# Four accumulator tiles of one bank each, and a rearranged start, in a Fourier-mixing and gated feed-forward kernel

## The chip, the cores and the metric

The kernel runs on one core of a Trainium2 chip. The metric is the device time of one execution in microseconds; a kernel's figure is the median of its runs. All times inside an execution are counted from the start of the profiled span.

## The reference

Eight sequences of 3008 tokens with 256 features go through a real Fourier transform over the tokens, a complex 256x256 product with bias, a soft threshold of real and imaginary part, and the inverse transform. The 24064 tokens that come out go through a feed-forward block with a sigmoid-gated unit, 256 to 2048 to 256.

```python
X = np.fft.rfft(x, axis=1)
Yr = Xr @ w_r - Xi @ w_i + b_r
Yi = Xr @ w_i + Xi @ w_r + b_i
Yr = np.sign(Yr) * np.maximum(np.abs(Yr) - lam, 0.0)   # Yi likewise, lam = 0.01
y = np.fft.irfft(Yr + 1j * Yi, n=x.shape[1], axis=1)
...
h = y @ w_in
g = h * (1.0 / (1.0 + np.exp(-1.702 * h)))
out = g @ w_out
```

The feed-forward weights come as float64, everything else is float32.

## The kernel before

**Numbers.** Most matmuls work on values split into a high and a low part of a shorter type (`fp32r`): `split` makes the high part on ACT (a cast) and the low part on DVE (a subtraction), and `mm3` multiplies high by high, high by low and low by high: lines L130, L131 and L132 of the profile. Where one factor is exact or a phase comes early ("plain"), an ordinary float32 matmul stands instead; it has two records in the trace.

**The spectral part of one batch** (`spectral`). 3008 is 64 times 47, and the transform goes in two steps. Stage A (L283, 16 blocks) transforms along 47; ACT copies each block out of PSUM (`aev`, L287) and SP stores it to a DRAM buffer `s1` (L288). Stage B (L312, 12 steps) reads rows `br` of `s1` back (L298) with a matrix `kr` from the input `kbs` (L297), transforms along 64, and ACT copies the outcome to `co`; DVE adds its two halves. Stage mix (L331) multiplies with `w_r`, `w_i` and their sum and difference (`wr`, `wd`); bias and threshold follow on DVE and ACT, and four DMAs turn the outcome into `yr`. Stage inv (L366) goes back along 64, `iev` is stored to a second DRAM buffer `s2`. At last `tokens` loads blocks `ur` of `s2` (L400), transforms back along 47 (L408) and splits the outcome into `th` and `tl`. A row of stage B needs all 16 blocks of stage A, a block of `tokens` needs all 12 steps of stage inv.

**The feed-forward part** (`Ffn`). A tile is 512 tokens; there are 47 tiles of 8 steps `q`. `up(q)` makes 12 matmuls of 512 columns into the PSUM tiles `pa` (four banks that all stages share), ACT applies the gated unit (`gb`, L440), ACT and DVE make seven combinations and their splits (`hb`, `lb`, `ht`, `lt`). `down(q)` makes 21 matmuls of 256 columns with seven combined weight blocks (a Strassen-like scheme, `ORDER`) into the accumulator `po`, one tile of four PSUM banks. After the last step `combine` reads it out with one ACT copy (L502, `o0` from bank 0) and DVE adds (L503 to L509); POOL does one add between (L507). The last tile has `combine_last` (L488 to L497), and for its last two steps plain matmuls (L477) with `gl`.

**The weights** (`weights(q)`, q from 0 to 7). POOL requests 512 KB of float64 (`wraw`, L192), and some ten ACT and DVE operations make float32 halves of it (`we`, `wm`, `wa`, then `wi_h`, `wi_l`, `wo_h`, `wo_l`).

**What sets the order.** The code is written as one program; a scheduler then sets the order on each engine by its own estimate of when each instruction could run, and every engine works its list off in order, SP its DMA requests too. `tc.issue_after(ins)` binds what stands in its block behind `ins` on `ins`'s engine alone. A tile of a pool is free again when all its readers are done. Batch 0 runs through at the start; blocks of stage A of batches 1 and 2 serve as `filler` between the first feed-forward steps; later batches are spread between the steps by a queue. `hold_clock(ins, n)` puts n matmuls with no use (L518) on PE behind `ins`. `split_constants` splits the constants `ka`, `ki`, `wf` that batches from 1 on need.

Of the kernel before, what the change touches and what calls it, by code (L numbers as in the profile page):

```python
# [9 lines left out]
F32 = mybir.dt.float32  # L10
# [4 lines left out]
AF = mybir.ActivationFunctionType  # L15
ALU = mybir.AluOpType
# [10 lines left out]
TOK, HT = 512, 256  # L27
# [78 lines left out]
def fourier_mix_then_gated_ffn(ctx: ExitStack, tc: tile.TileContext, x, w_r, w_i, b_r, b_i, w_in, w_out, pack, kbs, out):  # L106
    nc = tc.nc
# [21 lines left out]
    def mm3(ps, wh, wl, xh, xl, start=True, stop=True):  # L129
        nc.tensor.matmul(ps, lhsT=wh, rhs=xh, start=start, stop=False)  # L130
        nc.tensor.matmul(ps, lhsT=wh, rhs=xl, start=False, stop=False)  # L131
        nc.tensor.matmul(ps, lhsT=wl, rhs=xh, start=False, stop=stop)  # L132
# [5 lines left out]
    kz, fg, fk = kc[:96, 352:446], kc[:, 446:470], kc[:, 470:482]  # L138
    nlam = cst.tile([128, 1], F32, name="nlam")
    nc.vector.memset(nlam, -LAM)  # L140
    ka = cst.tile([96, 2, 96], F32R, name="ka")
    ki = cst.tile([128, 2, 2, 128], F32R, name="ki")
    bias = cst.tile([128, 2, D], F32, name="bias")
# [91 lines left out]
        else:  # L235
            split(wo_h[:, q], wo_l[:, q], t[:, 0:7])

    done_a, done_inv = [], []
    evacuated, stored, mixed, split_to = [], [], [], []


    def spectral(b, s2):
# [4 lines left out]
        xs, raw, zs, ys = {}, {}, {}, {}  # L247

        plain, plain_a = b == 0, b < 3

# [28 lines left out]
        def stage_a(q):  # L279

            ps = bank()
            if plain_a:
                done_a.append(nc.tensor.matmul(ps[:96], lhsT=ka32, rhs=xs.pop(q), start=True, stop=True).ins)  # L283
# [4 lines left out]
            stored.append(nc.sync.dma_start(s1w[:, 512 * q:512 * (q + 1)], ev).ins)  # L288

        def load_b(sp):  # L290
            if plain:
                kt = buf([128, 3, D], F32, "br0", tag=("zh", "zl")[sp % 2])
                t, k = kt[:, 0:2], kt[:, 2].rearrange("p (i n) -> p i n", i=2)
            else:
                t, k = buf2("br"), buf([128, 2, 2 * N1], F32, "kr")
            with tc.issue_after(stored[13]):
                nc.sync.dma_start(k, kbs[sp])  # L297
            nc.sync.dma_start(t, s1r[2 * sp:2 * sp + 2].rearrange("s p d -> p s d"))  # L298
            raw[sp] = t, k

        def stage_b(sp):

            ahead = 3 if plain else 1
            for n in range(0 if sp == 0 else sp + ahead, min(sp + ahead + 1, 12)):
                load_b(n)
            t, k = raw.pop(sp)
            co = buf([128, 2, 3, 128], F32, "co")
            pv = bank().rearrange("p (c v i n) -> p c v i n", c=2, v=2, i=2)
            for i in range(2):
                for c in range(2):  # L310
                    cs = slice(128 * c, 128 * c + 128)
                    nc.tensor.matmul(pv[:, c, :, i], lhsT=t[:, i, cs], rhs=k[:, i], start=True, stop=True)  # L312
# [73 lines left out]
            for n in range(4):  # L386
                load_x(n)

        return first, second, preload


    s2s, us, ytiles = {}, {}, {}
# [32 lines left out]
    class Ffn:  # L425
# [43 lines left out]

        def down(self, q):  # L470
            if q == 0:
                self.acc = ps_o.tile([128, 4, 2, HT], F32, name="po", tag="po")
            g = self.g.pop(q)
            for n, (a, t, bk, h) in enumerate(ORDER):
                start, stop = q == 0 and FIRST[bk] == n, q == NQ - 1 and LAST[bk] == n
                if not isinstance(g[t], tuple):
                    nc.tensor.matmul(self.acc[:, bk, h], lhsT=self.w32[q][:, a], rhs=g[t], start=start, stop=stop)  # L477
                else:
                    mm3(self.acc[:, bk, h], wo_h[:, q, a], wo_l[:, q, a], *g[t], start=start, stop=stop)
            if q == NQ - 1:  # L480
                (self.combine_last if self.k == NT - 1 else self.combine)()

        def combine_last(self):

            p = self.acc
            o0, o1, uv = buf2("o0"), buf2("o1"), buf2("uv")
            v = nc.vector
            nc.scalar.copy(o0, p[:, 0])  # L488
            v.tensor_tensor(uv[:, 0], p[:, 1, 0], o0[:, 0], ALU.add)
            nc.gpsimd.tensor_tensor(o0[:, 0], o0[:, 0], o0[:, 1], ALU.add)  # L490
            v.tensor_tensor(o0[:, 1], uv[:, 0], p[:, 1, 1], ALU.add)
            v.tensor_tensor(uv[:, 1], p[:, 2, 0], uv[:, 0], ALU.add)
            v.tensor_tensor(o0[:, 1], o0[:, 1], p[:, 2, 1], ALU.add)
            nc.sync.dma_start(out[self.k, :, 0], o0.rearrange("p h n -> p (h n)"))
            v.tensor_tensor(o1[:, 1], uv[:, 1], p[:, 1, 1], ALU.add)
            v.tensor_tensor(o1[:, 0], uv[:, 1], p[:, 3, 0], ALU.subtract)
            nc.scalar.dma_start(out[self.k, :, 1], o1.rearrange("p h n -> p (h n)"))  # L497

        def combine(self):
            p = self.acc  # L500
            o0, o1, uv = buf2("o0"), buf2("o1"), buf2("uv")
            nc.scalar.copy(o0, p[:, 0])  # L502
            nc.vector.tensor_tensor(uv[:, 0], p[:, 1, 0], o0[:, 0], ALU.add)  # L503
            nc.vector.tensor_tensor(uv[:, 1], p[:, 2, 0], uv[:, 0], ALU.add)
            nc.vector.tensor_tensor(o1[:, 0], uv[:, 1], p[:, 3, 0], ALU.subtract)
            nc.vector.tensor_tensor(o1[:, 1], uv[:, 1], p[:, 1, 1], ALU.add)
            nc.gpsimd.tensor_tensor(o0[:, 0], o0[:, 0], o0[:, 1], ALU.add)  # L507
            nc.vector.tensor_tensor(o0[:, 1], uv[:, 0], p[:, 1, 1], ALU.add)
            nc.vector.tensor_tensor(o0[:, 1], o0[:, 1], p[:, 2, 1], ALU.add)  # L509
            for e, o in enumerate((o0, o1)):  # L510
                nc.sync.dma_start(out[self.k, :, e], o.rearrange("p h n -> p (h n)"))

    def hold_clock(ins, count):

        with tc.issue_after(ins):
            o = ps_o.tile([128, 4, 2, HT], F32, name="po", tag="po").rearrange("p c h n -> p (c h n)")
            for _ in range(count):
                nc.tensor.matmul(o[:96, 0:446], lhsT=ka32, rhs=kc[:96, 0:446], start=True, stop=True)  # L518

# [7 lines left out]
    (first, second, _), (first1, queue, preload), (first2, queue2, _) = (spectral(b, new_s2(b)) for b in range(3))  # L527
    nextb = 2
    for n, (_, step) in enumerate(first + second):
        step()  # L530
        if n == len(first) - 1:
            later_constants()
        if n == len(first) - 1:
            hold_clock(done_a[-1], 4)
        if n == len(first) + 36:
            preload()
    with tc.issue_after(evacuated[15]):
        split_constants()
    filler = first1 + first2
    last_aev = evacuated[15]  # L540

    def fill(count):
        for _ in range(2 * count):
            if filler:
                filler.pop(0)[1]()

    def weights(q):
        with ExitStack() as held:

            for ins in ([last_aev] if q < 5 else mixed if q == 5 else first_tokens) if q else ():  # L550
                held.enter_context(tc.issue_after(ins))
            up_weights(q, q > 5)
            down_weights(q, q > 5)
# [12 lines left out]
    for u in range(3):  # L566
        load_u(u)
    with tc.issue_after(loaded[-1]):
        fill(4)
    hold_clock(done_inv[-1], 5)  # L570
    tokens_to(TOK)
    first_tokens = tuple(split_to)
    with tc.issue_after(loaded[2]), tc.issue_after(turned[-1]):
        fill(2)
    for q in range(6):
        weights(q)
    behind = total = None
    for n in range(NT * NQ):
# [4 lines left out]
            cur = Ffn(k)  # L583
        cur.up(q)
        fill(3)
        if not queue and nextb < NB:
            if nextb == 2:
                queue = queue2
            else:
                first, second, _ = spectral(nextb, new_s2(nextb))  # L590
                queue = first + [(4000, lambda: None)] + second
            nextb += 1
            total = None
# [52 lines left out]
```

## Time and profile before

| what | value |
|---|---|
| median of three runs | 2633.46 us (2631.92 to 2638.31) |
| the profiled execution, its own time | 2632.74 us |
| its span | 2630.6 us |
| PE busy in the span | 98% |
| DVE, ACT, POOL busy | 75%, 62%, 2% |
| mean granted PE clock | 0.992 of full speed |

The time of an execution is its span and some 2 us around it. A busy PE is not yet a PE at its peak: matmuls overlap in their pipeline, and at half the granted clock the same matmul is busy for longer. So the idle time of PE and the stretches at a low clock have to be read together.

### The profile page before, as it was taken

What the parts mean: (1) busy time and instruction counts of PE and PEld (TensorE: products, weight loads), DVE (VectorE), ACT (ScalarE), POOL (GpSimd) and SP (SyncE); (2) the same over time, 40 slices, a digit from 0 to 9 for tenths busy, and PEclk for the clock granted to TensorE, in tenths of its full rate; (3) what the DMA queues carried; (4) which work ended last, traced back from release to release, by engine and by line L of the source; (5) the groups of instructions that cost most, each with busy time, mean ns of one, the idle gap of its engine ahead of it and who ended that gap; (6) DMA issues with size and microseconds to landing.
All of it is one profiled execution on the core that took longest, in us unless ns stands there. A gap on an engine that the chain in (4) does not pass through costs nothing.

```text
span 2630.6 us, 42804 instructions
## 1 busy us (share of the span) xinstructions
PE 2589.7 (98%) x16520; PEld 2327.6 (88%) x16520; DVE 1967.4 (75%) x3219; ACT 1642.7 (62%) x2547; POOL 53.8 (2%) x71
## 2 busy tenths in 40 slices
PE   7899999999999999999999999999999999999998
PEld 4679999999899998999989999899998999999998
DVE  6767877777777777777777777778777777777676
ACT  5566666666666666666676666766667666655554
POOL 1000000000000000000000000000000000000000
PEclk8899999999999999999999999999999999999999
DMA  8652221111322223212241221322213122200000
GB/s 259 205 171 71 82 86 49 50 59 55 95 79 62 69 62 103 74 60 68 64 124 56 68 67 60 120 63 61 75 60 121 47 74 62 66 18 32 18 20 17
DMA packets 156075, 200.64 MB, mean 76 GB/s; under 512 B 18688, under 2 KB 105600, under 8 KB 155872
## 3 DMA queue, kind: packets, MB, share of 16 engines
q1 hardware_dynamic: 153360, 189.26, 23.7%
q0 software_dynamic: 2368, 8.39, 1.0%
q8 instruction: 130, 2.13, 0.4%
q14 instruction: 73, 0.60, 0.1%
q10 hardware_dynamic: 144, 0.26, 0.0%
HBM read 97.70 MB, written 74.97 MB: 66 GB/s over the span
## 4 chain that ended last, share of the span: by engine, by line
PE 90%; issue 7%; DMA 2%; DVE 1%; ACT 1%; POOL 0%; SPq 0%; POOLq 0%; DVEq 0%; ACTq 0%
PE pa L130 16%; PE pa L131 16%; PE pa L132 16%; PE po L130 11%; PE po L131 11%; PE po L132 11%; PE pa L408 4%; PE pa L312 3%; PE pa L283 1%; PE pa L331 1%; DMA wraw<-in_w_in 1%; DMA s<-aev 0%; PE pa L366 0%; DMA yr<-mv 0%; ACT gb L440 0%
## 5 line engine op out<-in xcount | busy, mean ns | idle before, releaser
L440 ACT ACTIVATE gb<-pa 128x512 f32<-128x512 f32 x752 | 447.0, 598 | 424.0 <-PE pa L132 421.4
L127 DVE TENSOR_TENSOR lt<-gt,ht 128x1024 fp32r<-128x1024 f32 x374 | 458.3, 1226 | 246.8 <-ACT ht L127 245.7
L130 PE MATMUL pa<-th,wi_h 128*128 128x512 f32 x1504 | 597.5, 397 | 2.9 <-ACT gb L440 2.1
L131 PE MATMUL pa<-tl,wi_h 128*128 128x512 f32 x1504 | 591.4, 393 | 0.0
L132 PE MATMUL pa<-th,wi_l 128*128 128x512 f32 x1504 | 588.1, 391 | 0.0
L127 ACT CAST ht<-gt 128x1024 fp32r<-128x1024 f32 x374 | 391.5, 1047 | 158.5 <-DVE gt L462 146.8
L131 PE MATMUL po<-lt,wo_h 128*128 128x256 f32 x1496 | 427.0, 285 | 0.0
L130 PE MATMUL po<-ht,wo_h 128*128 128x256 f32 x1496 | 425.1, 284 | 0.0
L132 PE MATMUL po<-ht,wo_l 128*128 128x256 f32 x1496 | 423.3, 283 | 0.0
L127 DVE TENSOR_TENSOR lb<-gb,hb 128x768 fp32r<-128x768 f32 x375 | 358.7, 957 | 43.2 <-ACT hb L127 41.0
L460 DVE TENSOR_TENSOR gt<-gb 128x512 f32<-128x512 f32 x374 | 261.7, 700 | 134.5 <-ACT gb L440 131.1
L127 ACT CAST hb<-gb 128x768 fp32r<-128x768 f32 x375 | 313.4, 836 | 69.2 <-PE po L132 62.3
L132 PEld LDWEIGHTS pa<-th,wi_l 128*128 128x128 f32 x1504 | 283.5, 188 | 57.3
L130 PEld LDWEIGHTS pa<-th,wi_h 128*128 128x128 f32 x1504 | 284.9, 189 | 52.0 <-ACT gb L440 3.3
L130 PE MATMUL po<-hb,wo_h 128*128 128x256 f32 x1125 | 327.5, 291 | 0.9 <-DVE o L509 0.9
L131 PEld LDWEIGHTS pa<-tl,wi_h 128*128 128x128 f32 x1504 | 284.7, 189 | 44.4 <-DVE wa L198 0.5
L131 PE MATMUL po<-lb,wo_h 128*128 128x256 f32 x1125 | 319.9, 284 | 0.0
L132 PE MATMUL po<-hb,wo_l 128*128 128x256 f32 x1125 | 319.0, 284 | 0.0
L132 PEld LDWEIGHTS po<-ht,wo_l 128*128 128x128 f32 x1496 | 285.7, 191 | 8.6 <-issue 1.7
L131 PEld LDWEIGHTS po<-lt,wo_h 128*128 128x128 f32 x1496 | 285.6, 191 | 8.7 <-issue 1.8
L130 PEld LDWEIGHTS po<-ht,wo_h 128*128 128x128 f32 x1496 | 285.5, 191 | 3.8 <-issue 1.3
L130 PEld LDWEIGHTS po<-hb,wo_h 128*128 128x128 f32 x1125 | 214.8, 191 | 10.1 <-issue 2.6
(123 smaller groups left out, 3780.0 us busy)
## 6 DMA issues: line engine op xcount, KB each, us to landing
s<-aev SPq DMA_DIRECT2D x128, 192.0 KB, 2.6
br<-s SPq DMA_DIRECT2D x96, 256.0 KB, 3.0
yr<-mv SPq DMA_DIRECT2D x384, 64.0 KB, 2.0
s<-iev SPq DMA_DIRECT2D x96, 256.0 KB, 2.3
ur<-s SPq DMA_DIRECT2D x128, 192.0 KB, 2.8
out<-o SPq DMA_DIRECT2D x93, 256.0 KB, 2.1
xr<-in_x SPq DMA_DIRECT2D x80, 192.0 KB, 3.1
kr<-in_kbs SPq DMA_DIRECT2D x84, 128.0 KB, 2.1
```

The lines of the kernel that those rows point to most:

```text
L127: return nc.scalar.copy(hi, src).ins, nc.vector.tensor_tensor(lo, src, hi.bitcast(F32), ALU.subtract).ins
L130: nc.tensor.matmul(ps, lhsT=wh, rhs=xh, start=start, stop=False)
L131: nc.tensor.matmul(ps, lhsT=wh, rhs=xl, start=False, stop=False)
L132: nc.tensor.matmul(ps, lhsT=wl, rhs=xh, start=False, stop=stop)
L283: done_a.append(nc.tensor.matmul(ps[:96], lhsT=ka32, rhs=xs.pop(q), start=True, stop=True).ins)
L312: nc.tensor.matmul(pv[:, c, :, i], lhsT=t[:, i, cs], rhs=k[:, i], start=True, stop=True)
L331: nc.tensor.matmul(ps, lhsT=z[:, 3 * c + v], rhs=wf32[v][:, c], start=c == 0, stop=c == 1)
L408: turned.append(nc.tensor.matmul(pv[:, c, 94 * j:94 * j + 94], lhsT=t[:, j, 128 * c:128 * c + 128], rhs=kz, start=True, stop=True).ins)
L440: nc.scalar.activation(o, ps.rearrange("p (h n) -> p h n", h=2), AF.Gelu_apprx_sigmoid)
L460: nc.vector.tensor_tensor(gt[:, 0:2], b12, gb[:, 0:3:2], ALU.subtract)
```

## The change

- The accumulator is four tiles of one bank, each with its own tag (`po0` to `po3`), where it was one tile of four banks. The fillers of `hold_clock` take `po0`.
- `load_b`: the first matrix of a batch is bound to a store of stage A of the same batch (number 13 of batch 0, number 15 of the others); each further matrix is bound behind the row request before it. In before all matrices were bound to batch 0's store 13.
- `preload_b`: rows 0 and 1 of batch 1 are requested when 12 or fewer filler steps are left.
- `split_constants` stands behind the last mixing operations of batch 0 (`mixed`, one on DVE and one on ACT), where it stood behind the last `aev` copy.
- `weights(1)` is bound to `aev` copy 11 in place of 15.
- 7 unused matmuls behind stage A for 4; 3 for 5 at the end of batch 0, now bound behind stage A blocks; three filler blocks for four at that place, bound behind the last stage inv; one for two after the first tokens.
- A one-element activation loads the gated unit's table at the start.

```diff
+    nc.scalar.activation(cst.tile([128, 1], F32, name="gelu_table"), nlam, AF.Gelu_apprx_sigmoid)
...
-            stored.append(nc.sync.dma_start(s1w[:, 512 * q:512 * (q + 1)], ev).ins)
+            mine.append(nc.sync.dma_start(s1w[:, 512 * q:512 * (q + 1)], ev).ins)
+            stored.append(mine[-1])
...
-            with tc.issue_after(stored[13]):
+            if sp == 0:
+                later.append(mine[13 if plain else 15])
+            with tc.issue_after(later[-1]):
                 nc.sync.dma_start(k, kbs[sp])
-            nc.sync.dma_start(t, s1r[2 * sp:2 * sp + 2].rearrange("s p d -> p s d"))
+            later.append(nc.sync.dma_start(t, s1r[2 * sp:2 * sp + 2].rearrange("s p d -> p s d")).ins)
...
+        def preload_b():
+            load_b(0)
+            load_b(1)
...
-                self.acc = ps_o.tile([128, 4, 2, HT], F32, name="po", tag="po")
+                self.acc = [ps_o.tile([128, 2, HT], F32, name="po", tag=f"po{i}") for i in range(4)]
...
-                    mm3(self.acc[:, bk, h], wo_h[:, q, a], wo_l[:, q, a], *g[t], start=start, stop=stop)
+                    mm3(self.acc[bk][:, h], wo_h[:, q, a], wo_l[:, q, a], *g[t], start=start, stop=stop)
...
-            hold_clock(done_a[-1], 4)
+            hold_clock(done_a[-1], 7)
...
-    with tc.issue_after(evacuated[15]):
+    with tc.issue_after(mixed[0]), tc.issue_after(mixed[1]):
         split_constants()
...
-            for ins in ([last_aev] if q < 5 else mixed if q == 5 else first_tokens) if q else ():
+            for ins in ([evacuated[11 if q == 1 else 15]] if q < 5 else mixed if q == 5 else first_tokens) if q else ():
...
     with tc.issue_after(loaded[-1]):
-        fill(4)
-    hold_clock(done_inv[-1], 5)
+        with tc.issue_after(done_inv[-1]):
+            fill(3)
+    hold_clock(done_a[-1], 3)
...
-        fill(2)
+        fill(1)
...
+        if preload_b and len(filler) <= 12:
+            preload_b()
+            preload_b = None
```

Lines shift by up to 12: stage A's L283 is L284 in the changed kernel, L298 is L302, L312 is L317, L366 is L371, L400 is L409, L408 is L417, L477 is L486, L518 is L527. The same instructions run as before, but for one unused matmul more and one activation in place of a second table load. What moves is seen at three places.

**SP, between stage A and stage B of batch 0.** Before: the last two stores `s_83<-aev`, the bias, five matrices (three of batch 0, two `kr` of batch 1), then four rows.

```order
L288 DMA s_83<-aev 96x512 x2
L154 DMA bias<-in_b_r 128x256
L155 DMA bias<-in_b_i 128x256
L297 DMA br_202<-in_kbs 128x256
L297 DMA br_205<-in_kbs 128x256
L297 DMA br_208<-in_kbs 128x256
L297 DMA kr<-in_kbs 128x256 x2
L298 DMA br_199<-s_83 128x2x256
L298 DMA br_202<-s_83 128x2x256
L298 DMA br_205<-s_83 128x2x256
```

The same place in the changed kernel:

```order
L289 DMA s_85<-aev 96x512 x2
L155 DMA bias<-in_b_r 128x256
L156 DMA bias<-in_b_i 128x256
L302 DMA br_204<-s_85 128x2x256
L301 DMA br_207<-in_kbs 128x256
L302 DMA br_207<-s_85 128x2x256
L301 DMA br_210<-in_kbs 128x256
L302 DMA br_210<-s_85 128x2x256
```

The first row stands right behind the bias, and each matrix behind the row before it; the two `kr` have moved far back.

**PE, from the end of batch 0 to the first feed-forward matmul.** Before: L366 is stage inv, L283 a filler block of batch 1, L518 the unused matmuls, L408 the tokens, L130 the first `up`.

```order
L366 MATMUL pa<-yr_582,kc 128x256 x2
L366 MATMUL pa<-yr_616,kc 128x256
L283 MATMUL pa<-xa,kc 96x512 x3
L366 MATMUL pa<-yr_616,kc 128x256
L518 MATMUL po<-kc 96x446 x5
L283 MATMUL pa<-xa,kc 96x512
L408 MATMUL pa<-kc,ur 128x94 x12
L283 MATMUL pa<-xa,kc 96x512 x2
L130 MATMUL pa<-th,wi_h 128x512
```

In the changed kernel:

```order
L371 MATMUL pa<-yr_587,kc 128x256 x2
L371 MATMUL pa<-yr_621,kc 128x256 x2
L284 MATMUL pa<-xa,kc 96x512 x3
L527 MATMUL po<-kc 96x446 x3
L417 MATMUL pa<-kc,ur 128x94 x12
L284 MATMUL pa<-xa,kc 96x512
L130 MATMUL pa<-th,wi_h 128x512 x2
```

The last matmul of stage inv no longer stands behind three filler blocks, no block stands ahead of the tokens, and one instead of two between them and the first `up`.

**PE, the end of the program.** Before, one accumulator (`po_27752`):

```order
L132 MATMUL po_27752<-hb_27991,wo_l_81 128x256
L477 MATMUL po_27752<-gl_27993,w32_27994 128x256 x4
L477 MATMUL po_27752<-gb_28022,w32_28040 128x256 x3
L477 MATMUL po_27752<-gl_28039,w32_28040 128x256 x4
L638 UNCONDITIONAL_BRANCH
```

In the changed kernel, with banks 0 to 3 as `po_27893` to `po_27896`:

```order
L486 MATMUL po_27895<-gb_28166,w32_28184 128x256
L486 MATMUL po_27894<-gl_28137,w32_28138 128x256
L486 MATMUL po_27894<-gl_28183,w32_28184 128x256 x2
L486 MATMUL po_27896<-gl_28137,w32_28138 128x256
L486 MATMUL po_27895<-gl_28183,w32_28184 128x256
L486 MATMUL po_27896<-gl_28183,w32_28184 128x256
L650 UNCONDITIONAL_BRANCH
```

Bank 0 takes no part in the last matmuls any more, and bank 1 ends three matmuls ahead of the end.

More of the change, by code (lines that the diff above doesn't have):

```diff
@@ L236, in down_weights @@
             split(wo_h[:, q], wo_l[:, q], t[:, 0:7])
-    done_a, done_inv = [], []
+    done_a, done_inv, later = [], [], []
     evacuated, stored, mixed, split_to = [], [], [], []
@@ L246, in spectral @@
         s2w = s2.rearrange("(s r) p j d -> s (r p j) d", r=2)
-        xs, raw, zs, ys = {}, {}, {}, {}
+        xs, raw, zs, ys, mine = {}, {}, {}, {}, []
         plain, plain_a = b == 0, b < 3
@@ L304, in stage_b @@
             for n in range(0 if sp == 0 else sp + ahead, min(sp + ahead + 1, 12)):
-                load_b(n)
+                if n not in raw:
+                    load_b(n)
             t, k = raw.pop(sp)
@@ L387, in preload @@
                 load_x(n)
-        return first, second, preload
+        def preload_b():
+            load_b(0)
+            load_b(1)
+        return first, second, preload, preload_b
     s2s, us, ytiles = {}, {}, {}
@@ L476, in down @@
                 if not isinstance(g[t], tuple):
-                    nc.tensor.matmul(self.acc[:, bk, h], lhsT=self.w32[q][:, a], rhs=g[t], start=start, stop=stop)
+                    nc.tensor.matmul(self.acc[bk][:, h], lhsT=self.w32[q][:, a], rhs=g[t], start=start, stop=stop)
                 else:
-                    mm3(self.acc[:, bk, h], wo_h[:, q, a], wo_l[:, q, a], *g[t], start=start, stop=stop)
+                    mm3(self.acc[bk][:, h], wo_h[:, q, a], wo_l[:, q, a], *g[t], start=start, stop=stop)
             if q == NQ - 1:
@@ L487, in combine_last @@
             v = nc.vector
-            nc.scalar.copy(o0, p[:, 0])
-            v.tensor_tensor(uv[:, 0], p[:, 1, 0], o0[:, 0], ALU.add)
+            nc.scalar.copy(o0, p[0])
+            v.tensor_tensor(uv[:, 0], p[1][:, 0], o0[:, 0], ALU.add)
             nc.gpsimd.tensor_tensor(o0[:, 0], o0[:, 0], o0[:, 1], ALU.add)
-            v.tensor_tensor(o0[:, 1], uv[:, 0], p[:, 1, 1], ALU.add)
-            v.tensor_tensor(uv[:, 1], p[:, 2, 0], uv[:, 0], ALU.add)
-            v.tensor_tensor(o0[:, 1], o0[:, 1], p[:, 2, 1], ALU.add)
+            v.tensor_tensor(o0[:, 1], uv[:, 0], p[1][:, 1], ALU.add)
+            v.tensor_tensor(uv[:, 1], p[2][:, 0], uv[:, 0], ALU.add)
+            v.tensor_tensor(o0[:, 1], o0[:, 1], p[2][:, 1], ALU.add)
             nc.sync.dma_start(out[self.k, :, 0], o0.rearrange("p h n -> p (h n)"))
-            v.tensor_tensor(o1[:, 1], uv[:, 1], p[:, 1, 1], ALU.add)
-            v.tensor_tensor(o1[:, 0], uv[:, 1], p[:, 3, 0], ALU.subtract)
+            v.tensor_tensor(o1[:, 1], uv[:, 1], p[1][:, 1], ALU.add)
+            v.tensor_tensor(o1[:, 0], uv[:, 1], p[3][:, 0], ALU.subtract)
             nc.scalar.dma_start(out[self.k, :, 1], o1.rearrange("p h n -> p (h n)"))
@@ L501, in combine @@
             o0, o1, uv = buf2("o0"), buf2("o1"), buf2("uv")
[L502 to L506, printed above, removed]
+            nc.scalar.copy(o0, p[0])
+            nc.vector.tensor_tensor(uv[:, 0], p[1][:, 0], o0[:, 0], ALU.add)
+            nc.vector.tensor_tensor(uv[:, 1], p[2][:, 0], uv[:, 0], ALU.add)
+            nc.vector.tensor_tensor(o1[:, 0], uv[:, 1], p[3][:, 0], ALU.subtract)
+            nc.vector.tensor_tensor(o1[:, 1], uv[:, 1], p[1][:, 1], ALU.add)
             nc.gpsimd.tensor_tensor(o0[:, 0], o0[:, 0], o0[:, 1], ALU.add)
-            nc.vector.tensor_tensor(o0[:, 1], uv[:, 0], p[:, 1, 1], ALU.add)
-            nc.vector.tensor_tensor(o0[:, 1], o0[:, 1], p[:, 2, 1], ALU.add)
+            nc.vector.tensor_tensor(o0[:, 1], uv[:, 0], p[1][:, 1], ALU.add)
+            nc.vector.tensor_tensor(o0[:, 1], o0[:, 1], p[2][:, 1], ALU.add)
             for e, o in enumerate((o0, o1)):
@@ L515, in hold_clock @@
         with tc.issue_after(ins):
-            o = ps_o.tile([128, 4, 2, HT], F32, name="po", tag="po").rearrange("p c h n -> p (c h n)")
+            o = ps_o.tile([128, 2, HT], F32, name="po", tag="po0").rearrange("p h n -> p (h n)")
             for _ in range(count):
@@ L526, in fourier_mix_then_gated_ffn @@
     assert NB > 2
-    (first, second, _), (first1, queue, preload), (first2, queue2, _) = (spectral(b, new_s2(b)) for b in range(3))
+    (first, second, *_), (first1, queue, preload, preload_b), (first2, queue2, *_) = (spectral(b, new_s2(b)) for b in range(3))
     nextb = 2
@@ L533, in fourier_mix_then_gated_ffn @@
         if n == len(first) - 1:
-            hold_clock(done_a[-1], 4)
+            hold_clock(done_a[-1], 7)
         if n == len(first) + 36:
             preload()
-    with tc.issue_after(evacuated[15]):
+    with tc.issue_after(mixed[0]), tc.issue_after(mixed[1]):
         split_constants()
     filler = first1 + first2
-    last_aev = evacuated[15]
     def fill(count):
@@ L589, in fourier_mix_then_gated_ffn @@
             else:
-                first, second, _ = spectral(nextb, new_s2(nextb))
+                first, second, *_ = spectral(nextb, new_s2(nextb))
                 queue = first + [(4000, lambda: None)] + second
```

## The prediction

> **What bounds the kernel now.** I read the page first, then windows over the span, then the order of time on PE, SP and ACT where the windows show idle PE.
>
> ```profile
> span 2630.6 us, 42804 instructions
> PE 2589.7 (98%) x16520; PEld 2327.6 (88%) x16520; DVE 1967.4 (75%) x3219; ACT 1642.7 (62%) x2547; POOL 53.8 (2%) x71
> ```
>
> PE is the bound, with some 41 us idle. The windows (stretch, length, busy time by engine, granted PE clock, DMA share, GB/s) tell where:
>
> ```profile
> 25.00:50.00 25.00, 16.07 (x60) 11.07 (x59) 18.21 (x39) 12.18 (x23) 2.17 (x3) 0.74 0.80 260
> 100.00:125.00 25.00, 20.36 (x55) 11.87 (x55) 11.30 (x25) 9.01 (x19) 0.80 (x2) 0.70 0.51 164
> 225.00:2600.00 2375.00, 2368.97 (x15467) 2160.37 (x15466) 1795.69 (x2887) 1499.42 (x2302) 39.02 (x45) 1.00 0.22 66
> 2600.00:2632.00 32.00, 23.67 (x149) 21.31 (x147) 16.51 (x28) 9.18 (x13) 0.72 (x1) 0.95 0.05 17
> ```
>
> From 225 to 2600 us PE idles 6.0 us at full clock: there is nearly nothing to be had. Two early stretches have both idle time and a clock near 0.7. Finer windows put half clock at these places:
>
> ```profile
> 34.40:44.60 10.20, 4.02 (x17) 3.90 (x18) 8.47 (x22) 2.87 (x6) 1.18 (x2) 0.50 0.86 280
> 99.20:102.60 3.40, 3.26 (x7) 1.61 (x6) 3.23 (x7) 1.60 (x3) 0.00 (x0) 0.50 0.80 255
> 112.90:126.50 13.60, 13.11 (x37) 9.25 (x38) 5.76 (x12) 6.40 (x14) 1.07 (x2) 0.50 0.52 165
> 198.20:201.60 3.40, 3.40 (x19) 3.40 (x18) 2.94 (x8) 1.90 (x3) 0.72 (x1) 0.50 0.49 147
> ```
>
> PE's order of time (start, length, work, idle before it) shows the idle ahead of each:
>
> ```profile
> 40.58 3.75 PE L312 MATMUL pa<-br 128*128 128x128 f32 x16 [8.93 <-ACT wm L199]
> ...
> 98.67 2.85 PE L366 MATMUL pa<-yr,kc 128*128 128x256 f32 x6 [2.27 <-DMA yr<-mv]
> 101.32 3.39 PE L283 MATMUL pa<-xa,kc 96*96 96x512 f32 x6
> 104.55 0.60 PE L366 MATMUL pa<-yr,kc 128*128 128x256 f32 x2
> 104.99 3.90 PE L518 MATMUL po<-kc 96*96 96x446 f32 x10
> 113.39 1.99 PE L283 MATMUL pa<-xa,kc 96*96 96x512 f32 x2 [4.50 <-DMA xa<-in_x]
> 115.18 5.27 PE L408 MATMUL pa<-kc,ur 96*128 96x94 f32 x24
> 120.24 3.62 PE L283 MATMUL pa<-xa,kc 96*96 96x512 f32 x4
> 122.88 1.42 PE L130 MATMUL pa<-th,wi_h 128*128 128x512 f32 x1
> ...
> 197.23 2.86 PE L312 MATMUL pa<-kr,br 128*128 128x128 f32 x16 [2.19 <-DMA br<-s]
> ```
>
> Idle of 2.2 us is followed within 1.2 us by a half-clock stretch of 3.4 us, 4.5 us idle by one of 13.6 us. What is saved ahead of 225 us moves all that follows, since PE is full there.
>
> **Part 1, stage A to stage B of batch 0.** SP's queue (start, length, requests):
>
> ```profile
> 29.30 0.30 SPq L288 DMA_DIRECT2D s<-aev  x1
> ...
> 30.64 1.39 SPq L297 DMA_DIRECT2D br<-in_kbs  x3
> 32.07 1.03 SPq L297 DMA_DIRECT2D kr<-in_kbs  x2
> 33.15 4.15 SPq L298 DMA_DIRECT2D br<-s  x4
> ```
>
> The last store and the first row take from issue to landing, in this order:
>
> ```profile
> DMA to landing us min/median/max: 2.8/2.8/2.8
> DMA to landing us min/median/max: 7.3/7.3/7.3
> ```
>
> The store lands at 32.1, the first row at 33.15 + 7.3 = 40.4, and PE starts at 40.58: it waits for the row, though the trace names an ACT operation that ends at the same moment. Moving five matrices behind the row saves 33.15 - 32.1 = 1.05 us of issue, and 5 x 128 KB at the 260 GB/s of that window, 2.5 us, in the queue; the two overlap only in part. I take 3: with the row at 37.4 both terms count nearly whole. The bounds are 1 (issue alone) and 5 (with the half-clock loss of 34.40:44.60, 4.02 us busy at half speed, gone too). The three more fillers cost 3 x 0.78 us of idle PE (3.90 us for 10 records, two to a matmul); they end near 34 and are covered as long as the row lands after that. The constants leave this stretch; their five casts and subtractions free ACT and DVE, and the weights move up into the gap, which is a rival below. **-3**, range -5 to +1.
>
> **Part 2, end of batch 0 to the first `up`.** ACT's order of time at this place, one constant's cast (line group: count, busy, mean ns), and the page's DMA times (KB, us to landing):
>
> ```profile
> 100.27 0.59 ACT L373 COPY iev<-pa 128x512 f32<-128x512 f32 x1 [0.58 <-ACT wm L199]
> ...
> 105.23 0.59 ACT L373 COPY iev<-pa 128x512 f32<-128x512 f32 x1 [3.85 <-issue]
> ```
>
> ```profile
> L127 ACT CAST wf_h<-wd 128x512 fp32r<-128x512 f32 x2 | 1.2, 618 | 0.2 <-DVE wd L158 0.2
> ```
>
> ```profile
> s<-iev SPq DMA_DIRECT2D x96, 256.0 KB, 2.3
> ur<-s SPq DMA_DIRECT2D x128, 192.0 KB, 2.8
> wraw<-in_w_in POOLq DMA_DIRECT2D x6, 512.0 KB, 6.3
> ```
>
> On the clock of before: the last stage-inv matmul moves ahead of three filler blocks, 104.55 - 101.32 = 3.2 us earlier, so it ends near 101.9. ACT isn't free then: the five casts now stand ahead of the last three `iev` copies, at most 5 x 0.62 = 3.1 us, about 2.5 since two of them are small. The second last copy, at 100.27 before, moves to 102.8, and the last one follows at once: it ends near 103.5 in place of 105.82. The chain gains 2.3 us, not 3.2. Store and load behind it stay, 2.3 and 2.8: the first `ur` lands near 108.6. Before, by the same 5.1 us, it was there near 110.9, but the tokens began at 115.18, since a filler block that waited for its `xa` stood ahead of them. PE in between: three blocks (3.39) to 105.3, six filler records (2.34) to 107.6, then 1.0 us idle, under the 2.2 us that a clock drop needed. The 24 token records took 5.27 us at half clock; at full clock it is 2.6 if nothing waits, and I take 3.0, since they go in three groups of which each waits for a load. One block (half of 120.24's two, at full clock 0.9) and 0.4 for the last cast of `th` bring the first `up` to 108.6 + 3.0 + 0.9 + 0.4 = 112.9 against 122.88: 10.0. Two filler blocks fewer are done by then, 2 x 0.9 = 1.8 of work moved to later; for it, the 3.6 us of `up` matmuls up to 126.5 run at full clock, 1.8 gained. **-10**, range -12 to -4 (the low end with a clock drop, below). The five subtractions on DVE move with the casts; DVE is busy for 11.30 of 25 us here, which covers them. If it doesn't, `tl` is late next.
>
> **Part 3, batch 1's first rows.** Requested some filler blocks earlier, they are there when PE reaches L317: 2.19 us idle go, and most of the 1.7 us that 198.20:201.60 loses. **-3**, range -3.9 to 0. What holds two `br` longer is two of seven `w2` buffers; `aev` copies and `ur` loads would wait next.
>
> **Part 4, the end.**
>
> ```profile
> 2621.78 1.89 PE L477 MATMUL po<-gl,w 128*128 128x256 f32 x8
> ...
> 2623.71 0.59 ACT L488 COPY o<-po 128x512 f32<-128x512 f32 x1 [6.55 <-PE po L477]
> ...
> 2624.83 0.72 POOL L490 TENSOR_TENSOR o<-o 128x256 f32<-128x256 f32 x1 [35.13 <-DVE uv L489]
> 2625.59 0.42 DVE L491 TENSOR_TENSOR o<-uv,po 128x256 f32<-128x256 f32 x1 [0.83 <-POOL o L490]
> ...
> 2626.92 0.41 DVE L496 TENSOR_TENSOR o<-uv,po 128x256 f32<-128x256 f32 x1
> ```
>
> One accumulator tile made the copy wait for the very last matmul; from there to the last add's end (2627.33) it is 3.66 us. With bank 0 done early the copy is past; bank 1 is done three plain matmuls (3 x 0.43) ahead of the end, so the first add and POOL's 0.72 lie beside matmuls. Left behind the last matmul are about four adds: 1.6 us. **-2**, range -3 to 0.
>
> **Part 5, the rest.** The steady stretch is worth at most its 6.0 us of idle and costs what new waits bring; two rows of the waits (total, times, longest) bear on it:
>
> ```profile
> PEld pa L130 <- ACT gb L440: 3.8, 4, 1.1
> PE po L130 <- DVE o L509: 0.9, 1, 0.9
> ```
>
> The accumulator made PE wait once in 46 changes of tile, so freeing it bank by bank gains 0.9; the other waits hang on the new order, which may drop or add some. **0**, range -5 to +6. The table load lay beside matmuls at 125 and now lies in ACT's first idle time: **0**, its 1.3 us at most.
>
> **Sum.** -3 - 10 - 3 - 2 = -18 against the profiled execution's 2632.74 (its span of 2630.6 and 2.1 around it): 2614.7. The median of the runs is 0.7 above that execution, so 2615.4; I say **2615**.
>
> **Rivals.** *The clock drops again before the tokens.* If the `ur` blocks come 1.2 us later than worked out, the idle is 2.2 us. For: tokens go in three groups that each wait for a load. Price: 13.1 us at half speed, up to 6.5 us: 2621.5. The Trainium skill, in TensorE: Matmul & The Clock Gate, section HAM oscillation, puts the limit at idle gaps of some 3.4 us; by that this rival is out, and part 1 gains about a microsecond more, 2614. The trace disagrees: 2.19 and 2.27 us were enough.
>
> *The weights crowd the start.* `weights(1)` bound to copy 11 lets its conversions run between the last copies, so POOL's next two requests, each 512 KB, go out near 27 and 29 us, not 32.5 and 38.4, and ACT and DVE now have those conversions queued ahead of `co`, so stage mix waits for a landing of 6.3 us. Against: before, the same requests fell into the same gap. Price: part 1 turns from -3 to +4, 2622. The Trainium skill, DMA: Bandwidth & Descriptors, section Issuing engines are not separate DMA queues, says that transfers of all issuers share 16 engines; so does the trace (DMA share 0.80 at 25 to 50 us). By it alone 1 MB at 260 GB/s would cost 4 us, the same 2622.
>
> *Given back later.* The feed-forward part starts 13 us earlier, but PE could wait in the first tile for `weights(6)`, whose loads go out only behind the first tokens, or for x blocks of the fillers. For: the idle at 113.39 was such a wait. Against: step 6 is several steps away, and PE had no wait of that kind behind 122.88. Price: 12 of the 13 us of parts 1 and 2, so 2627, about no measurable change.
>
> *Slower: the accumulator's banks.* The scheduler, freed bank by bank, puts the next tile's `down` closer behind `combine`, and PE waits at each of 46 changes for the copy (0.59) and up to six adds of 0.42. It decides from 18 / 46 = 0.4 us each; at 1 us each it is 2615 + 46 = 2661. Against: bank 0, which `down` takes first, needs the copy alone.
>
> **Chances.** Forecast 0.52, its own range 2609 to 2620; clock 0.17; weights 0.12; given back 0.12; banks 0.07. What a measurement can tell from no change is 0.3%, 7.9 us: faster is under 2625.6. Forecast, clock and weights lie there, less a little for the edges: 0.80. Same 0.13, slower 0.07. The range takes in clock and weights and the near half of given back: 2607 to 2627.
>
> **What would show it.** Part 1: L317 first starts near 37.5. Part 2: the first L139 (`up`) near 110 of the new span, tokens right behind the fillers with under 2 us idle, clock 1.00 there. Part 3: no idle at the first `kr` step. Part 4: the ACT copy starts before PE's last matmul ends, and under 2.2 us lie between that end and the last add. Wrong: idle over 6 us in the steady stretch with `po` as the one that waits, or half clock beyond 105.

## The result, and the profile after

The changed kernel takes 2612.38 us (median of 4 runs, 2609.64 to 2614.76) against 2633.59 us before (4 runs, 2631.92 to 2638.31): a ratio of 0.9916, with a 95% interval of 0.9901 to 0.9931. That is 21.2 us; forecast were 18.6 from the median (2633.6 to 2615), 18 in terms. Five more runs of the same file gave 2614.15; the median of all nine is 2613.18, and that is what the experiments below are held against. The profiled execution took 2611.57 us, its span is 2609.8 us.

The page's first lines of the kernel after, and its windows (stretch, length, busy time by engine, granted PE clock, DMA share, GB/s):

```profile
span 2609.8 us, 42914 instructions
PE 2583.2 (99%) x16522; PEld 2323.2 (89%) x16522; DVE 1967.4 (75%) x3219; ACT 1642.8 (63%) x2547; POOL 55.4 (2%) x71
```

```profile
25.00:50.00 25.00, 18.19 (x47) 9.68 (x47) 20.14 (x44) 13.48 (x24) 2.89 (x4) 0.73 0.89 284
100.00:125.00 25.00, 23.27 (x94) 14.67 (x94) 20.37 (x43) 18.34 (x38) 1.07 (x2) 0.93 0.71 227
125.00:225.00 100.00, 100.00 (x580) 81.35 (x579) 73.48 (x131) 65.64 (x108) 2.92 (x5) 1.00 0.47 141
225.00:2600.00 2375.00, 2372.84 (x15500) 2166.00 (x15499) 1798.83 (x2892) 1503.09 (x2304) 40.54 (x45) 1.00 0.22 65
```

From 100 to 125 us the clock is 0.93 where it was 0.70. From 125 to 225 us PE never idles. From 225 to 2600 us idle PE fell from 6.0 to 2.2 us, in a stretch that the prediction had written off. At 25 to 50 us there is no gain to be seen. PE's order of time after (start, length, work, idle before it):

```profile
25.45 7.05 PE L284 MATMUL pa<-xe,kc 96*96 96x512 f32 x8 [0.45 <-ACT aev L288]
32.35 5.40 PE L527 MATMUL po<-kc 96*96 96x446 f32 x14
41.73 1.32 PE L317 MATMUL pa<-br 128*128 128x128 f32 x8 [3.98 <-DMA br<-s]
...
102.72 3.36 PE L284 MATMUL pa<-xa,kc 96*96 96x512 f32 x6
105.92 2.41 PE L527 MATMUL po<-kc 96*96 96x446 f32 x6
109.06 3.42 PE L417 MATMUL pa<-kc,ur 96*128 96x94 f32 x24 [0.73 <-DMA ur<-s]
112.32 1.03 PE L284 MATMUL pa<-xa,kc 96*96 96x512 f32 x2
112.96 0.62 PE L130 MATMUL pa<-th,wi_h 128*128 128x512 f32 x1
...
189.91 1.95 PE L317 MATMUL pa<-kr,br 128*128 128x128 f32 x16
```

Stage B begins at 41.73, later than before (40.58); counted from the end of stage A it is 9.2 us, before 11.9, but stage A itself ended 3.9 us later. The end of batch 0 goes as forecast: fillers, held matmuls, 0.73 us idle, tokens at full clock, first `up` at 112.96 (before 122.88). The first `kr` step waits for nothing. The end of the span, in order of time on PE, ACT and DVE:

```profile
2599.42 0.59 ACT L497 COPY o<-po 128x512 f32<-128x512 f32 x1 [2.78 <-PE po L486]
...
2601.95 2.75 PE L486 MATMUL po<-gl,w 128*128 128x256 f32 x12
...
2605.77 0.41 DVE L502 TENSOR_TENSOR o<-o,po 128x256 f32<-128x256 f32 x1
```

The copy runs while PE still works, and from the last matmul (2604.70) to the last add's end (2606.18) it is 1.48 us, before 3.66.

Cut at two marks, the end of the last stage mix and the first `up`, the span splits like this in the profiles (stage A's end, first stage B matmul and first `up` as in PE's order of time; the last column is the span less the first `up`):

| profile | stage A ends | first stage B | last mix ends | mix to `up` | `up` to end |
|---|---|---|---|---|---|
| before | 28.66 | 40.58 | 93.81 | 29.06 | 2507.7 |
| after | 32.51 | 41.73 | 95.03 | 17.93 | 2496.8 |
| after, again | 29.52 | 39.34 | 92.27 | 19.49 | 2498.3 |
| banks alone (on before) | 25.82 | 40.13 | 91.85 | 31.94 | 2496.7 |
| fillers alone (on before) | 29.94 | 41.91 | 94.32 | 18.23 | 2509.3 |
| banks and fillers (on before) | 26.22 | 40.84 | 92.49 | 18.55 | 2496.0 |
| one accumulator (in after) | 28.78 | 38.97 | 95.42 | 20.18 | 2509.9 |
| fillers as before (in after) | 28.96 | 38.27 | 93.27 | 30.02 | 2495.4 |
| start as before (in after) | 31.16 | 41.51 | 96.03 | 20.02 | 2494.9 |

So the 20.8 us between the two spans are +1.2 up to the last mix, -11.1 from there to the first `up`, and -10.9 behind it. The two gains belong to two parts of the change, and the table shows which: the fillers make the column from the last mix to the first `up`, the accumulators the column behind it.

### The profile page after: what moved, and what is told of

Read it like the earlier page. It is cut to its first block, busy times and chain, and to the rows that moved or that the text cites. A ratio compares the mean times of both kernels' runs of the same rounds, so it can differ in the third digit from the quotient of the medians.

```text
span 2609.8 us, 42914 instructions
## 1 busy us (share of the span) xinstructions
PE 2583.2 (99%) x16522; PEld 2323.2 (89%) x16522; DVE 1967.4 (75%) x3219; ACT 1642.8 (63%) x2547; POOL 55.4 (2%) x71
## 4 chain that ended last, share of the span: by engine, by line
PE 96%; DMA 2%; issue 2%; DVE 0%; ACT 0%; SPq 0%; POOL 0%; POOLq 0%; DVEq 0%; ACTq 0%
PE pa L130 17%; PE pa L131 17%; PE pa L132 17%; PE po L130 12%; PE po L131 12%; PE po L132 12%; PE pa L417 4%; PE pa L317 3%; PE pa L284 1%; PE pa L336 1%; DMA s<-aev 1%; DMA wraw<-in_w_in 0%; DMA yr<-mv 0%; DMA br<-s 0%; PE pa L371 0%
## 5 line engine op out<-in xcount | busy, mean ns | idle before, releaser
L130 PE MATMUL pa<-th,wi_h 128*128 128x512 f32 x1504 | 592.3, 394 | 0.4 <-ACT aev L288 0.4
L131 PE MATMUL po<-lt,wo_h 128*128 128x256 f32 x1496 | 408.5, 286 | 0.0
L132 PE MATMUL po<-ht,wo_l 128*128 128x256 f32 x1496 | 405.1, 283 | 0.0
L130 PE MATMUL po<-ht,wo_h 128*128 128x256 f32 x1496 | 354.6, 284 | 0.0
L130 PEld LDWEIGHTS pa<-th,wi_h 128*128 128x128 f32 x1504 | 284.1, 189 | 45.6 <-ACT aev L288 0.9
L130 PE MATMUL po<-hb,wo_h 128*128 128x256 f32 x1125 | 321.4, 294 | 0.0
L130 PEld LDWEIGHTS po<-ht,wo_h 128*128 128x128 f32 x1496 | 259.1, 190 | 10.7 <-issue 2.3
L131 PEld LDWEIGHTS po<-lb,wo_h 128*128 128x128 f32 x1125 | 214.4, 191 | 11.1 <-DVE lb L127 1.8
```

## The experiments

All were timed in five rounds beside the kernel before, whose medians in the four groups were 2633.49, 2633.50, 2632.74 and 2635.03 us.

**After, once more.** No edit.

> The changed kernel as it is, once more, on the chip of the next three. In its first profile the eight loads of x land by 22.7 us and stage A ends at 32.4 us, against 18.8 and 28.7 us before, though the requests are the same. Theory 'chance' (the DMA rate of the first 25 us differs from one execution to the next): in this profile the last x load lands at some other time, 18 to 23 us, and the first L317 moves with it. Theory 'table' (the table load or the order behind it delays x): again 22 to 23 us. Median 2612, within 3, by both.

Measured: 2614.15 us (2611.81 to 2615.29). "Chance" holds. The eight loads of x from issue to landing, before, after and after again:

```profile
DMA to landing us min/median/max: 4.2/11.1/14.1
DMA to landing us min/median/max: 4.4/13.5/16.6
DMA to landing us min/median/max: 4.1/11.7/13.6
```

The same requests took up to 14.1, 16.6 and 13.6 us, so the late end of stage A in the first profile after is chance for the larger part. (Not all of it need be: the last of the eight requests starts at 4.9 to 6.2 us in the nine profiles with the early table load, at 4.5 to 5.2 in the five without.) But this profile also shows what the first did not:

```profile
106.49 4.55 PE L417 MATMUL pa<-kc,ur 96*128 96x94 f32 x24 [2.21 <-DMA ur<-s]
...
120.65 1.03 PE L417 MATMUL pa<-kc,ur 96*128 96x94 f32 x8
```

```profile
108.00:111.00 3.00, 3.00 (x16) 3.00 (x16) 2.10 (x3) 1.44 (x3) 0.00 (x0) 0.50 1.03 373
114.00:117.00 3.00, 3.00 (x6) 1.61 (x5) 2.04 (x5) 1.20 (x4) 0.00 (x0) 0.50 0.39 124
```

Idle of 2.21 us ahead of the tokens, then half clock until past 117 us. From the first to the next tokens it is 14.16 us; in the first profile, at full clock, the same work lies between 109.06 and this row:

```profile
119.23 1.03 PE L417 MATMUL pa<-kc,ur 96*128 96x94 f32 x8
```

That is 10.17 us: the prediction's clock rival comes true in some executions and costs 4.0 us.

**The weights back behind copy 15**, and **the constants back behind copy 15.**

```diff
-for ins in ([evacuated[11 if q == 1 else 15]] if q < 5 ...
+for ins in ([evacuated[15]] if q < 5 ...
```

```diff
-    with tc.issue_after(mixed[0]), tc.issue_after(mixed[1]):
+    with tc.issue_after(evacuated[15]):
         split_constants()
```

> The changed kernel with weights(1) bound to aev copy 15 again, as before; all else changed. The prediction's rival 'the weights crowd the start': the 1 MB that POOL requests at 29.8 and 32.1 us goes out behind the last stores, so the last store lands about 3 us after its request instead of 5.6, the first row follows, and the first L317 starts 3 to 4 us sooner after the end of stage A (9.4 us in the profile after, so 5.5 to 6.5): total 2609. Rival 'the weights are needed early': what is saved there is lost behind it, since conversions then stand between the first co copies and stage mix waits for wo/wi work or the first down waits: 2612 to 2614.

> The changed kernel with the constants split behind aev copy 15 again (five casts, 2.5 us on ACT, in the gap between stage A and stage B). Theory: they lie in idle time there and no longer stand ahead of the last iev copies, so nothing is lost at the start, and the end of batch 0 gains 0 to 2 us: 2610 to 2613. Rival (the reason for the move): they push the weights' conversions and co copies back, and the stalls of 0.4 to 0.7 us in stages B and mix come back, 2 to 4 us in sum: 2614 to 2616.

Measured: 2612.17 us (2611.11 to 2616.28) and 2613.60 us (2612.31 to 2616.32), neither apart from 2613.18. Why the early weights cost nothing shows in two landings, the last store of stage A and the first row; first after, then with the weights back:

```profile
DMA to landing us min/median/max: 5.6/5.6/5.6
DMA to landing us min/median/max: 2.7/2.7/2.7
```

```profile
DMA to landing us min/median/max: 2.1/2.1/2.1
DMA to landing us min/median/max: 5.7/5.7/5.7
```

POOL's next two requests of weights start at 29.79 and 32.09 us in the one and at 34.59 and 38.60 in the other, so the same bytes lie ahead of the store in the one and ahead of the row in the other: 8.3 and 7.8 us together. Stage B begins 8.7 us behind stage A with the weights back, not 5.5 to 6.5 as the first theory had it. SP's queue after, the last bias and the first row, shows that the row's request waits for that landing (33.15 + 5.6 = 38.8), not for requests ahead of it:

```profile
34.05 0.47 SPq L156 DMA_DIRECT2D bias<-in_b_i  x1
38.91 0.38 SPq L302 DMA_DIRECT2D br<-s  x1
```

**The fillers at the end of batch 0 as before, in the changed kernel.**

```diff
-        with tc.issue_after(done_inv[-1]):
-            fill(3)
-    hold_clock(done_a[-1], 3)
+        fill(4)
+    hold_clock(done_inv[-1], 5)
...
-        fill(1)
+        fill(2)
```

> The changed kernel with the filler blocks and held matmuls at the end of batch 0 as before: fill(4) not bound to the last stage-inv, five held matmuls behind it, fill(2) behind the tokens. Theory (part 2 of the prediction): the order of the fillers makes nearly all of the 10 us, by the idle ahead of the tokens and the half clock behind it: first up near 122 us, a half-clock stretch over 10 us long, total 2620 to 2623. Rival (the late constants, matrices and rows free ACT and SP, and the order matters little): first up near 115, total 2613 to 2616.

Measured: 2617.35 us (2615.57 to 2620.45), 4.2 over 2613.18, less than the theory and more than the rival. The profiled execution, the slowest of its five (2620.45), fits the theory: first `up` at 123.29 behind a wait of 3.40 us and half clock, 8.7 us more span than the second profile of after (2618.7 to 2610.0). The other four runs took 2615.57 to 2617.63, at a mean granted clock of 0.994 to 0.995 where the profiled one had 0.993. A thousandth of 2618 us is 2.6 us, so by this estimate a shorter time at half clock makes 3 to 5 us, which is most of the difference; where it was shorter isn't known.

**The accumulators alone, on the kernel before.** The edit is `po` as four tiles in place of one; nothing else.

```diff
-self.acc = ps_o.tile([128, 4, 2, HT], F32, name="po", tag="po")
+self.acc = [ps_o.tile([128, 2, HT], F32, name="po", tag=f"po{i}") for i in range(4)]
```

> The kernel before with one part of the change: four accumulators of one bank each in place of one tile of four. Theory A (the prediction's part 4 alone): the end gets 2.2 us shorter (3.66 to 1.48 us from the last matmul to the last add) and the steady stretch stays with 6.0 us of idle PE: 2633.5 - 2 = 2631. Theory B: the accumulator as one tile also shaped the order in the steady stretch, and its waits (3.8 us on gb copies, 2.1 and 3.5 us at the xh step with a half-clock dip, 0.9 on o) go with it, as they went in the profile after: idle PE from 225 us to 2600 us falls from 6.0 to under 3, total 2626 to 2628.

Measured: 2622.28 us (2618.92 to 2625.79), ratio 0.9957 (0.9944 to 0.9971): 11.2 us, beyond theory B. The windows of the steady stretch, before and with the banks alone:

```profile
225.00:2590.00 2365.00, 2358.97 (x15402) 2151.20 (x15401) 1788.45 (x2875) 1493.80 (x2294) 39.02 (x45) 1.00 0.22 66
```

```profile
225.00:2590.00 2365.00, 2363.31 (x15454) 2157.64 (x15454) 1793.49 (x2884) 1500.00 (x2299) 42.97 (x45) 1.00 0.22 66
```

Idle PE falls from 6.0 to 1.7 us, though nothing in that stretch was changed but the accumulator. PE's order of time at one change of tile tells how, before:

```profile
1235.98 0.28 PE L132 MATMUL po<-ht,wo_l 128*128 128x256 f32 x1
...
1240.76 0.39 PE L132 MATMUL pa<-th,wi_l 128*128 128x512 f32 x1
1241.84 0.50 PE L130 MATMUL pa<-th,wi_h 128*128 128x512 f32 x1 [0.69 <-ACT gb L440]
...
1245.37 0.28 PE L130 MATMUL po<-hb,wo_h 128*128 128x256 f32 x1
```

and the same change after:

```profile
1217.97 0.28 PE L132 MATMUL po<-ht,wo_l 128*128 128x256 f32 x1
...
1220.94 1.03 PE L417 MATMUL pa<-kc,ur 96*128 96x94 f32 x8
1221.75 0.37 PE L130 MATMUL po<-hb,wo_h 128*128 128x256 f32 x1
```

with the last add of the readout on DVE, before and after:

```profile
1242.29 0.41 DVE L509 TENSOR_TENSOR o<-o,po 128x256 f32<-128x256 f32 x1
```

```profile
1223.27 0.41 DVE L518 TENSOR_TENSOR o<-o,po 128x256 f32<-128x256 f32 x1
```

Before, the next tile's `down` stood behind the whole readout. PE got 8.4 us of other work in between, all of it into the four `pa` banks, and waited 0.69 us until ACT had emptied one. After, `down` begins 1.5 us before the last add, and the stretch without `po` is 3.5 us, before 9.1. Over the steady part, 36 such stretches of over 8 us stand in the profile before and none after; five of the six waits of over 0.4 us before lie in stretches of over 7 us without `po`, and the sixth is the wait for `o` itself. That the blocked accumulator made the scheduler choose this order is read from the two orders; the runs show that the waits come and go with the accumulator, here and in the next run. The Trainium skill, in Perfetto Trace Analysis, section Matmuls, asks for PSUM banks in rotation so that the readout of one lies beside the next group's matmuls; this trace agrees, and shows the price of the opposite where it isn't looked for, on `pa`.

**One accumulator again, in the changed kernel.** The reverse edit.

> The changed kernel with one accumulator tile of four banks again, all else changed. Theory A: the end alone is lost, 2613 + 2 = 2615, idle PE in the steady stretch stays near 2 us. Theory B: the steady waits return, idle PE near 6 us and a half-clock dip: 2618 to 2621.

Measured: 2622.04 us (2620.31 to 2627.30), 8.9 over 2613.18: theory B, a little beyond its end. The profiled execution is one of two near 2627.3; the other three took 2620.3 to 2622.0. Its idle PE from 225 to 2590 us is 7.8 us. Waits of the steady stretch (total, times, longest) that came back, the first two as they were before, the third longer (before 0.9):

```profile
PEld pa L130 <- ACT gb L449: 3.8, 4, 1.1
PE pa L130 <- ACT xh L127: 2.1, 1, 2.1
PE po L130 <- DVE o L519: 2.1, 1, 2.1
```

**Batch 1's rows not requested early.** `preload_b` isn't called.

> The changed kernel without the earlier request of batch 1's first two rows. By the prediction's part 3 the wait at the first kr step comes back, 2.2 us idle and 1.7 us of half clock behind it: PE busy 125 to 225 us falls from 100.0 to about 97.8, total 2613 + 3 to 4 = 2616 to 2617. Rival: by the other moves the rows are there anyway: no idle, 2613.

Measured: 2615.50 us (2610.99 to 2617.61), 2.3 over 2613.18, with ranges that overlap. This profiled execution has no idle at the `kr` step:

```profile
194.95 1.05 PE L317 MATMUL pa<-kr,br 128*128 128x128 f32 x8
```

Its row landed at 194.52, 0.4 us ahead of the matmul; with the early request it landed at 181.19, 8.7 us ahead. The profile bears out the rival and the median leans to the theory. Other profiles without the early request side with the rival: the idle ahead of this step, 2.19 us before, is 1.69 with the banks alone, 0.50 with the fillers alone and none with both, and no half clock follows in any of the three. So the wait goes by the other parts; whether the early request adds anything stays unsettled.

**The fillers alone, on the kernel before.**

> The kernel before with one part of the change: the fillers and held matmuls at the end of batch 0 as in the changed kernel. Part 2 of the prediction as a whole: first up near 113 instead of 122.9, total 2623.5. By the run with the fillers set back, which lost 4 us in the median (8.7 between two profiled executions), 2629, with an idle of 2.2 us or more and a half-clock stretch ahead of the tokens still there.

Measured: 2624.18 us (2622.39 to 2625.44), ratio 0.9964 (0.9952 to 0.9977): 9.3 us, next to part 2's 10.

```profile
105.70 2.41 PE L518 MATMUL po<-kc 96*96 96x446 f32 x6
108.68 1.99 PE L408 MATMUL pa<-kc,ur 96*128 96x94 f32 x16 [0.57 <-DMA ur<-s]
...
112.55 0.85 PE L130 MATMUL pa<-th,wi_h 128*128 128x512 f32 x2
```

The tokens stand right behind the fillers, with the constants still split early: their move is no part of this gain.

**The start as before, in the changed kernel.** Matrices ahead of rows, four held matmuls, weights and constants behind copy 15, no early table load.

> The changed kernel with everything ahead of stage B of batch 0 as before: matrices ahead of rows, four held matmuls instead of seven, weights(1) and the constants behind aev copy 15, no early table load. By the prediction's part 1 (-3): 2613 + 3 = 2616, and from the end of stage A to the last group of twelve stage-inv records 65 us as before, against 62.5 and 62.8 in the two profiles of the changed kernel. Rival (the weights and the constants, each set back alone, moved the total by under 2 us): no change, 2613 to 2614, since what stage B gains is eaten by the wait for the stage-inv rows behind it.

Measured: 2612.36 us (2610.55 to 2613.30): the rival. The stretch that the theory names did grow: from the end of stage A to the end of the last stage mix it is 64.9 us, 65.2 before, 62.5 and 62.8 in the two profiles of the changed kernel. The total did not follow. All of part 1 together is worth nothing that can be measured.

**Six held matmuls ahead of the tokens; and twelve behind stage A as well.**

```diff
-    hold_clock(done_a[-1], 3)
+    hold_clock(done_a[-1], 6)
```

```diff
-            hold_clock(done_a[-1], 7)
+            hold_clock(done_a[-1], 12)
```

> The changed kernel with six held matmuls instead of three ahead of the first tokens (three more, 2.4 us). In most profiles so far PE idled 2.2 to 2.9 us there and ran the next 10 to 12 us at half clock, in two it idled 0.7 us and kept its clock. Theory (idle of about 2.2 us costs the clock there): idle under 1 us, full clock from the tokens on, and 4 us saved in each execution that had the drop: median 2610 to 2611, spread smaller. Rival (the clock follows the idle over a longer stretch, the waits for yr at 97 us too, so the drop stays; or the six matmuls end behind the ur block and delay it): 2613 to 2615.

> As the run with six, and twelve held matmuls instead of seven behind stage A of batch 0 (five more, 3.9 us of idle PE covered ahead of the first row). Theory: stage B starts at full clock, so its first matrices and mixes up to 10 us behind it go at full speed: 1 to 2 us saved, 2608.5 to 2610. Rival: the first steps of stage B and mix wait for rows and for co, not for PE, so the clock there is worth nothing, or the held matmuls end behind the row: same as the run with six, or 1 us more.

Measured: 2611.24 us (2609.62 to 2612.20) and 2609.59 us (2608.88 to 2612.98). PE's order of time and a window with six:

```profile
104.50 4.65 PE L527 MATMUL po<-kc 96*96 96x446 f32 x12
108.99 2.81 PE L417 MATMUL pa<-kc,ur 96*128 96x94 f32 x24
```

```profile
114.00:117.00 3.00, 3.00 (x12) 1.66 (x11) 2.79 (x7) 2.76 (x7) 1.00 (x2) 1.00 0.35 120
```

No idle, 2.81 us for the tokens, full clock where the second profile of after had 0.50, as the theory has it. With twelve the idle ahead of the first row falls to 0.75 us:

```profile
39.68 1.13 PE L317 MATMUL pa<-br 128*128 128x128 f32 x8 [0.75 <-DMA br<-s]
```

The clock from 39 to 50 us is 0.84 in this profile, 0.69 and 0.73 with seven: stage B starts at full clock, but 3.4 us of half clock still follow from 42.5 us on, so this theory holds in part. The kernel with both lies 3.6 us under the changed kernel's 2613.18 and 23 under before (ratio 0.9913, 0.9899 to 0.9926). The 3.6 are 0.14%, with ranges that overlap, so the size isn't secured. That the clock drops less shows in more than the two profiles: the mean granted clock of the nine runs with six (four of them with twelve too) is 0.996 to 0.998, of the nine of the changed kernel 0.994 to 0.996.

**Accumulators and fillers, on the kernel before.** The two edits together.

> The kernel before with two parts of the change, the four single-bank accumulators and the fillers at the end of batch 0. Alone they took 11.2 and 9.3 us off. If they add up and the rest of the change is worth nothing measurable: 2633.5 - 20.5 = 2613. If batch 1's rows are worth what their run said (2.3 us) and act here too: 2615 to 2616. If the two overlap: 2617 or more.

Measured: 2612.49 us (2608.87 to 2614.84), ratio 0.9922 (0.9909 to 0.9936). 11.2 and 9.3 add up to 20.5; measured are 20.6 by the ratio and 22.5 between the two medians of this group (2635.03 before), as expected of two parts that don't overlap. By its ratio the kernel is level with the changed one (0.9916, again 0.9924): everything else in the change together is worth nothing measurable, with intervals that would let some 3 us pass unseen.

## Why the prediction was right, and where not

The time lies inside the range and 2.6 us under the forecast, but that the sum came out right is in part luck: parts 1 and 3 (6 us together) brought nothing of their own that can be measured, and part 5, put at 0, brought about as much.

**Part 1 (-3) failed.** Its first step, "Moving five matrices behind the row saves 1.05 us of issue and 2.5 us in the queue", came out about right in sum: the row landed in 2.7 us where it took 7.3, the store ahead of it in 5.6 where it took 2.8, and SP, whose next request was the row, waited for that store until 38.91. Together with the issue, stage B began 2.7 us sooner behind stage A (9.2 us for 11.9; 9.8 in the second profile). So part of what was taken from the row's queue was put ahead of the store, as the weights rival had it; its price of +7 against the forecast was too high. The step that failed is "What is saved ahead of 225 us moves all that follows": with the start as before the total is the same (2612.36, so 0 measured). By the end of the last mix the profiles with the changed start lie at 92.3 to 95.6 us, those with the old one at 91.9 to 96.0; where the gain is lost isn't isolated. The landmark "L317 first starts near 37.5" was missed at 41.73 and 39.34, and 41.73 itself was in good part chance (x loads, 22.7 us for the last landing against 18.8).

**Part 2 (-10) held.** First `up` was forecast at 112.9 on the time scale of before, 19.1 us behind the last mix. It came at 112.96 and 111.76 in the two profiles, but counted from the last mix it is 17.9 and 19.5, and 18.2 with the fillers alone; those alone gave 9.3 us, though with the shorter idle at the first `kr` step in it. The reason was the one given, the tokens no longer behind a filler block that waits. The constants' casts, which had a place in the working, don't matter: the fillers alone do it without them. The clock rival (0.17) was underrated: four of the nine profiles with the new fillers and three held matmuls idle 2.1 to 2.9 us at this place, and all four run on at half clock. The 1.0 us of forecast idle was too little for four executions in nine.

**Part 3 (-3)** was right in the trace (no idle, no half clock at the first `kr` step), but not in the cause that it gave: the wait is gone without the early request too, with the fillers and the banks together. The 2.3 us by the medians are within the spread.

**Part 4 (-2) held**: 3.66 to 1.48 us, with 0.4 us more behind it, 1.8.

**Part 5 (0) is the term that was mis-sized.** Its step was "The accumulator made PE wait once in 46 changes of tile, so freeing it bank by bank gains 0.9; the other waits hang on the new order". They hung on the accumulator: the waits named `gb` and `xh` were the readout's cost, moved to `pa` by an order made around a blocked `po`. Measured: idle 6.0 to 1.7 us with the banks alone, and the half-clock stretch behind the longest wait (granted clock 0.60 from 1020 to 1024 us, a loss of 1.6) gone: 5.9 us, a little outside the range of -5 to +6. With the end it is 8 us of the 11.0 by which the profile with the banks alone is shorter behind the first `up`; some 2 more are idle and half clock ahead of 225 us, and about 1 is not accounted for. The medians give 9 to 11. The new order has a wait of its own:

```profile
2031.91 0.38 PE L131 MATMUL po<-lb,wo_h 128*128 128x256 f32 x1 [1.62 <-DVE lb L127]
```

It is from the first profile after, and stands in all eleven profiles with four accumulators.

The "slower" rival had the mechanism right and its sign wrong: `down` did move closer behind `combine`, and no wait of PE over 0.4 us names the readout any more. "Given back later" didn't happen in the changed kernel (no idle from 125 to 225 us); with the fillers alone a part of it did, 2.4 us of idle between 127 and 160 us.

## What to carry to other kernels

A wait is put down to what came last; when an order was made by a scheduler, ask also why PE was doing that work there, and look for stretches in which one resource isn't touched. An accumulator that is read out bank by bank was worth making as many tiles as banks: as one tile its next use waited for the last reader, and the order around it paid in places that don't name it. Test a change of many parts by adding single parts to the kernel before as well as by taking them out: here two parts made the whole gain, and a total that fitted hid that two others made none.

## What was not expected of the hardware

Identical loads at the start land at very different times: the last of the eight x loads at 18.8 to 22.7 us in the profiles, and the two profiles at these ends have stage A end 3.9 us apart. How much of the spread of some 5 us between runs this makes is not shown. The end of stage A goes with the clock as well: in two profiles the clock was full up to it (25.8 and 26.2 us), in the other twelve 3.4 or 6.8 us of half clock lay ahead of it, and it came at 28.7 to 32.5. And the clock's limit is not one length of idle: 2.16 to 2.91 us ahead of the tokens was followed by half clock in four profiles of four, 1.10 us or less in one of five. The same wait of 1.62 us for `lb` was followed by 3.4 us of half clock in four profiles of eleven (0.64 from 2033 to 2037 us in the first profile after, 1.00 in the second). Before, the half-clock stretches ahead of 2600 us were 6.8, 10.2, 3.4, 13.6, 3.4 and 3.4 us, that is one to four times 3.4. The Trainium skill, in TensorE: Matmul & The Clock Gate, section What's actually happening, describes a free-running window of 3.4 us that watches activity; the lengths agree with it, while the idle limit of some 3.4 us in its section HAM oscillation does not fit these traces.
